# Attention, a feed-forward layer and capacity routing in one kernel: the float64 weights get a clock of their own

## The chip, the cores and the metric

One core of a Trainium2 chip runs the whole program. The metric is device time in microseconds for one execution, measured three times. TensorE multiplies matrices, VectorE, ScalarE and GpSimd do elementwise work, and SyncE issues most transfers; the profile calls them PE, DVE, ACT, POOL and SP, and the loading of TensorE's weights PEld.

## What is computed

```python
# attention: (4, 8, 1152, 64), query rows averaged in pairs -> 576 rows per head
q_pool = q.reshape(B, H, S // 2, 2, D).mean(axis=3)
scores = scale * np.matmul(q_pool, k.transpose(0, 1, 3, 2))
attn = softmax(scores);  x = np.matmul(attn, v)        # 32 heads -> x (2304, 512)
# feed-forward; moe_w_in and moe_w_out are float64
h = np.maximum(x @ w_in, 0.0);  x2 = h * h @ w_out     # 512 -> 2048 -> 512
# routing: 2304 tokens, 8 experts, capacity 288, largest logit first
logits = x2 @ w_gate
# then per expert: relu(x2[mask] @ w1[e]) @ w2[e]
```

## The kernel before

**Stages.** The 32 heads run one after the other (`Attention`, until about 758 us); the hidden layer of a batch of 8 heads runs between the steps of the next batch (`batch_h`), the last one alone (`last_h`, to 836 us). Then `Second` multiplies by w_out (72 groups of 12 products, `Second.product`), with the routing threaded between its products (`phase2`, to about 1085 us), and last come the eight experts (`MoE.run`). Products are made in two or three float32r parts of a high and a low half, which is why most tensors exist twice.

**A head** is 18 steps. Step g makes one score tile four steps ahead (`score`, L271: two products L278 and L279, then the exponential on ScalarE, L282). `events` (L355) hangs the preparation of later heads on steps by the table `AT` (L44): `q_sum` on GpSimd (L187), `q_high` on ScalarE (four copies a head, L195), `q_low` and `k_low` on GpSimd (L201, L178), transposes on TensorE (`k_turn`, `q_turn`) with casts by ScalarE or VectorE (L207, L225, L246), and 15 `peak` products (L263) with a maximum by VectorE each (L265). At a head's last step `av` (L294) emits 18 value products (L307, two records each) and the row sums, and behind them ScalarE copies the results out of two PSUM banks (L322, L324), the sums go to DRAM and back as a row (L327 to L340), and four to five steps later GpSimd normalises the head (`norm`, L485). Every engine takes its instructions strictly in the order of emission.

**Row sums.** For heads below `ADD_HEADS` = 11 TensorE sums the exponentials with 18 thin products (L319, 36 records); from head 11 on GpSimd adds the nine tiles up (`total`, L286, 16 additions L292 per head) and TensorE needs 2 (L313, 4 records).

**Float64 weights.** `F64.load` (L79) takes 64 parts of 128x256 values. Each is loaded (L87), then decoded by VectorE (L90, L96, L105) and ScalarE (L93, L99, L102), each piece hung on its own later step by `AT["f0"]` to `AT["f5"]`. A part of w_in is then split (ScalarE L433, GpSimd L437 twice); a part of w_out is turned on TensorE (L452), copied (L453), stored (L456), and every second one multiplied with the gate (L462). `between(g)` (L616) starts one part every `EVERY` = 4 steps from step `FROM` = -37, so that the last starts at step 215, in head 11. The work of the hidden layer starts `LAG` = 22 steps behind its batch (L620).

**PSUM.** The tiles named wx share three banks (`px`), scores another three, and h two. The value products, the row sums, transposes, peaks, the turned w_out and the gate all take wx.

**Routing.** The gate's logits of a half batch are summed in `ls` (`Half.logits`, L526) and stored to DRAM in four pieces (L540). `Routing.init` (L693) loads them back in three pieces (L699) and turns them with 18 products (L700, 36 records). `route` (L976) is a generator: each number that it yields is a count of w_out products to let pass, `START` = 36 before `init`, `FIRST` = 32 before the first digit of each of 5 iterations, and 16 or 8 elsewhere. A digit's counting products (L751) need VectorE's tile `G` (L740).

Of the kernel before, what the change touches and what calls it, by code (L numbers as in the profile page):

```python
# [10 lines left out]
F32 = mybir.dt.float32  # L11
# [3 lines left out]
AF = mybir.ActivationFunctionType  # L15
# [7 lines left out]
NQ = S // 2  # L23
# [10 lines left out]
EPS = 1e-9  # L34
LAG = 22
FROM = -37
EVERY = 4.0
ADD_HEADS = 11
LOGS = 3
# [5 lines left out]
AT = dict(lq=-55, qs=-43, lk=-50, qh0=-41, qh1=-41, ql=-38, kh0=-39, kh1=-37, kl=-36, kt0=-28, kt1=-28, kt2=-25,  # L45
          qt0=-25, t2=-22, pk=-23, lv=-12, qt1=-6, qt2=-6, total=5, recip=8, spread=9, norm=14,
          high=0, wlow=4, turn=3, keep=4, gate=5, f0=9, f1=9, f2=9, f3=11, f4=11, f5=14)
TL, TA = 1, 5
ITERS = 5
START, FIRST, FAST, SLOW, LAST = 36, 32, 8, 16, 14  # L50
ROUNDS = N // 48, 48, E
# [61 lines left out]
class Attention:  # L113
# [7 lines left out]
    def __init__(self, ctx, tc, cm, q, k, v, scratch, emit, px, ph, yp):  # L121
# [18 lines left out]
        self.st = {}  # L140
        self.now = 0
        self.later = []
        self.y, self.rb = {}, {}
# [45 lines left out]
    def q_high(self, n, i):  # L189
        d = self.st[n]  # L190
        qs = d["qs"]
        if i == 0:
            d["q1"] = self.q1[0]
        for p, c in self.PARTS:
            self.nc.scalar.activation(d["q1"][p, c, i * 64:(i + 1) * 64], qs[p, c], AF.Copy)  # L195

# [97 lines left out]
    def av(self, n):  # L294
# [26 lines left out]
        for hf in range(2):  # L321
            nc.scalar.activation(y[mine, hf * HQ:(hf + 1) * HQ], A[hf * 64:(hf + 1) * 64, :HQ], AF.Copy)  # L322
        row = self.w1.tile([128, HQ], F32, name="row")
        nc.scalar.activation(row, t[:, :HQ], AF.Copy, bias=EPS / parts)  # L324
        rc = self.w2.tile([96, 2, 6], F32, name="rc")
        for j in range(parts):
            nc.sync.dma_start(rc[:, j, :], row[j * 32:j * 32 + 65:64])  # L327
        for c in range(9):
            del d["P", c]

        def total():
            if parts == 2:
                nc.gpsimd.tensor_tensor(rc[:, 0], rc[:, 0], rc[:, 1], op=OP.add)

        def recip():
            nc.vector.reciprocal(rc[:, 0], rc[:, 0])

        def spread():
            nc.sync.dma_start(self.scratch[n:n + 1, :], rc[:, 0])
            nc.sync.dma_start(rb[mine, :], bass.AP(tensor=self.scratch.tensor,  # L340
                                                   offset=self.scratch.offset + n * NQ,
                                                   ap=[[0, 64], [1, NQ]]))

        self.at(AT["total"], total)
        self.at(AT["recip"], recip)
        self.at(AT["spread"], spread)
        if odd:
            for k, f in self.emit(pr, y, rb):
                self.at(k, f)
            del self.y[pr], self.rb[pr]  # L350

    def at(self, k, f):
        self.later.append((self.now + k, f))

    def events(self, n):  # L355
# [15 lines left out]

    def run(self, heads, between):
# [7 lines left out]
        while g < end or self.later:  # L380
            self.now = g
            if 0 <= g < end and g % L == L - 1:
                self.av(g // L)
            if g >= ORDER_FROM:
                between(g)
            if 0 <= g + self.AHEAD < end:
                self.score(*divmod(g + self.AHEAD, L))
            for t in [x for x in self.later if x[0] <= g]:
                self.later.remove(t)
                t[1]()  # L390
            for f, *a in todo.get(g, ()):
                f(*a)
            if g < ORDER_FROM:
                between(g)
            g += 1


@with_exitstack
def fused_kernel(ctx, tc, q, k, v, w_in, w_out, w_gate, w1, w2, out, dbg=None, upto=9):
# [98 lines left out]
    class Half:  # L498


        def __init__(self, b, hf, eng):
            self.tok = slice(b * NQ + hf * HQ, b * NQ + (hf + 1) * HQ)
            self.eng = eng
            self.X, self.group = [], []

        def product(self, p, f, parts):
# [19 lines left out]
        def logits(self, f0):  # L526

            lg = px.tile([128, 512], F32, name="wx")
            if f0 == 0:
                self.ls = hp.tile([128, HQ], F32, name="ls", bufs=1)  # L530
# [5 lines left out]
            else:  # L536
                nc.vector.tensor_tensor(ls, lg[:, :HQ], ls, op=OP.add)
            if f0 == NF - 4:
                for i in range(4):
                    nc.sync.dma_start(lgs[E * i:E * i + E, self.tok], ls[32 * i:32 * i + E])  # L540
# [27 lines left out]
    def last_h(b, es, beside, ahead):  # L568
# [15 lines left out]
        for hf in range(2):  # L584
            m = H[hf]
            for f in range(NF):
# [22 lines left out]
    with ExitStack() as ea:  # L609
        ea.enter_context(tc.manual_schedule())  # L610
        att = Attention(ea, tc, cm, q, k, v, rs_scr, emit_x, px, ph_, yp)
        raw = ea.enter_context(tc.tile_pool(name="raw", bufs=1))
        f64 = F64(tc, raw, att.at)
        parts, taken = setup(f64, raw), 0

        def between(g):  # L616
            nonlocal work, taken
            while taken * EVERY <= g - FROM and next(parts, 0) is None:
                taken += 1
            b, r = divmod(g - LAG, H * 18)  # L620
# [6 lines left out]

        att.run(NH, between)
        for _ in work:
# [16 lines left out]
class Routing:  # L646
    def __init__(self, ctx, tc, cm, lgs, psum):
# [44 lines left out]

    def init(self):  # L693
# [199 lines left out]
class Second:  # L893


    def __init__(self, ctx, tc, h2s, wos, x2s):
# [4 lines left out]
        self.hp = ctx.enter_context(tc.tile_pool(name="h2p", bufs=3, side="right"))  # L901
        self.px = ctx.enter_context(tc.tile_pool(name="x2_ps", bufs=2, space=PS, side="right"))
        self.woh = wp.tile([128, NF, DM], R, name="woh")
        self.wol = wp.tile([128, NF, DM], R, name="wol")
# [63 lines left out]
def phase2(ctx, tc, cm, sec, lgs, x2s, dbg, w1, w2, out, upto):  # L968
    nc = tc.nc
    mo = MoE(ctx, tc, cm, x2s, w1, w2, out)  # L970
    with ExitStack() as es:
# [4 lines left out]
        def route():  # L976
            yield START
            rt.init()
            for _ in range(ITERS):
# [216 lines left out]
```

## Time and profile before

| What | Value |
|---|---|
| median of 3 runs | 1330.46 us (1329.3 to 1331.21) |
| the profiled execution's own time | 1329.09 us |
| its span, first to last instruction | 1327.3 us |
| mean granted TensorE clock | 0.979 |
| busy PE / DVE / ACT / POOL | 1244.9 / 720.5 / 703.1 / 657.4 us |
| heads, end of the last one's sums | about 758 us |
| transfers | 155.57 MB, 117 GB/s in the mean |

A matmul's record holds its whole way through the array, and the next one overlaps it; so TensorE's busy share is high even where it is held up, and it is read together with the waits and with the spacing of the starts. Where a wait is shown, `<-` names the instruction that ended it. A timeline row is: start, length, engine, line, operation, tiles, count, and in brackets the idle time before it.

### The profile page before, as it was taken

The page shows a single profiled execution, that of the slowest core. Times are in us where ns is not written, and L with a number is a line of the kernel's source. Part 1 is how long each engine was busy: PE and PEld are TensorE (multiplying, and loading weights), DVE is VectorE, ACT ScalarE, POOL GpSimd, SP SyncE. Part 2 cuts the span into 40 slices and gives each one's busy share as a digit, 9 for nine tenths or more (in the row PEclk, how much of TensorE's full clock was granted, in tenths as well). Part 3 has the DMA queues.
Part 4 walks back from the last instruction along what each step waited for, and adds up shares of the span by engine and source line. Part 5 has one row for each costly group of instructions (what it writes and reads, how often), then busy time and mean ns, then how long its engine had stood idle before and what let it go on. Part 6 is the DMA issues. An engine that isn't in the chain of part 4 may idle for free. (4 is left out here: it accounts for less than half of the span.)

```text
span 1327.3 us, 25135 instructions
## 1 busy us (share of the span) xinstructions
PE 1244.9 (94%) x9033; PEld 1046.9 (79%) x9033; DVE 720.5 (54%) x1654; ACT 703.1 (53%) x1816; POOL 657.4 (50%) x930
## 2 busy tenths in 40 slices
PE   5898888989899999999999999999999979999997
PEld 4666665778688788887887889777777759999997
DVE  6867586666554445454544011178877714655552
ACT  5767675767566666566666556132322214454541
POOL 4332333356777878878877543366655301221211
PEclk9999999999999999999999999899999979999999
DMA  5444344443232323232322144444343314555531
GB/s 169 126 122 145 108 141 116 113 143 108 73 95 81 96 82 96 82 95 74 103 82 60 46 156 162 122 120 135 119 143 120 112 44 160 189 197 189 194 132 36
DMA packets 135096, 155.57 MB, mean 117 GB/s; under 512 B 17878, under 2 KB 95958, under 8 KB 134966
## 3 DMA queue, kind: packets, MB, share of 16 engines
q1 hardware_dynamic: 131750, 144.21, 35.7%
q0 software_dynamic: 3072, 9.44, 2.3%
q8 instruction: 73, 1.20, 0.4%
q14 instruction: 57, 0.47, 0.1%
q10 hardware_dynamic: 144, 0.26, 0.1%
HBM read 111.46 MB, written 32.87 MB: 109 GB/s over the span
## 5 line engine op out<-in xcount | busy, mean ns | idle before, releaser
L265 DVE TENSOR_REDUCE mx<-wx 128x1 f32<-128x384 f32 (+1 forms) x424 | 229.4, 551 | 244.9 <-PE wx L263 242.7
L282 ACT ACTIVATE P<-sc 128x288 f32<-128x288 f32 x576 | 225.1, 410 | 75.7 <-PE sc L279 68.6
L292 POOL TENSOR_TENSOR ss<-ss,P 128x288 f32<-128x288 f32 x294 | 229.3, 805 | 21.1 <-ACT P L282 20.6
L278 PE MATMUL sc<-M,T 128*128 128x288 f32 x576 | 178.3, 310 | 1.6 <-ACT P L282 1.4
L279 PE MATMUL sc<-M,t 128*128 128x288 f32 x576 | 171.6, 298 | 2.7 <-DVE M L246 2.6
L263 PE MATMUL wx<-T,M 128*128 128x384 f32 (+1 forms) x424 | 149.4, 352 | 7.6 <-ACT T L207 3.2
L935 POOL TENSOR_TENSOR hl<-h,hh 128x256 fp32r<-128x256 f32 x130 | 101.7, 804 | 109.6 <-ACT hh L933 106.0
L307 PE MATMUL wx<-P,vf 128*64 128x288 f32 x1152 | 147.7, 411 | 0.8 <-DVE mx L265 0.8
L512 PE MATMUL h<-xh,wih 128*128 128x288 f32 x448 | 140.1, 313 | 0.0
L512 PE MATMUL h<-xl,wih 128*128 128x288 f32 x448 | 134.2, 300 | 5.4 <-POOL xl L495 5.3
L512 PE MATMUL h<-xh,wil 128*128 128x288 f32 x448 | 132.9, 297 | 1.4 <-POOL wil L437 1.4
L307 PEld LDWEIGHTS wx<-P,vf 128*64 128x64 f32 x1152 | 80.3, 138 | 58.5 <-DVE mx L265 5.4
L278 PEld LDWEIGHTS sc<-M,T 128*128 128x128 f32 x576 | 109.5, 190 | 20.4 <-issue 7.4
L958 PE MATMUL x2p<-woh,hh 128*128 128x512 f32 x288 | 117.6, 408 | 0.0
L958 PE MATMUL x2p<-woh,hl 128*128 128x512 f32 x288 | 117.4, 408 | 0.0
L933 ACT ACTIVATE hh<-h 128x512 fp32r<-128x512 f32 x72 | 45.3, 630 | 135.7 <-PE x2p L958 130.6
L958 PE MATMUL x2p<-wol,hh 128*128 128x512 f32 x288 | 117.0, 406 | 0.0
L279 PEld LDWEIGHTS sc<-M,t 128*128 128x128 f32 x576 | 109.6, 190 | 4.9 <-DVE M L246 4.6
L512 PEld LDWEIGHTS h<-xh,wih 128*128 128x128 f32 x448 | 84.9, 190 | 10.2 <-issue 10.2
L178 POOL TENSOR_TENSOR ks<-raw,ks 128x192 fp32r<-128x192 f32 x93 | 55.5, 619 | 73.7 <-ACT ks L171 73.7
L512 PEld LDWEIGHTS h<-xl,wih 128*128 128x128 f32 x448 | 84.9, 189 | 8.8 <-POOL xl L495 8.7
L1070 POOL DMA_INDIRECT xg<-x_scr,ix x24 | 27.0, 1125 | 130.4 <-PE ept L1083 88.5
(199 smaller groups left out, 2937.8 us busy)
## 6 DMA issues: line engine op xcount, KB each, us to landing
eraw<-in_moe_w_dram SPq DMA_DIRECT2D x56, 512.0 KB
h_scr<-h2st SPq DMA_DIRECT2D x64, 288.0 KB
h<-h_scr SPq DMA_DIRECT2D x72, 256.0 KB
raw<-in_k_dram SPq DMA_DIRECT2D x32, 288.0 KB
t<-T SPq DMA_DIRECT2D x32, 288.0 KB
vf<-in_v_dram SPq DMA_DIRECT2D x32, 288.0 KB
raw<-in_q_dram SPq DMA_DIRECT2D x32, 256.0 KB
words<-in_moe_w_in_dram SPq DMA_DIRECT2D x32, 256.0 KB
```

The lines of the kernel that those rows point to most:

```text
L178: eng.tensor_tensor(ks[:, c, 0:64], d["kn"][:, c], ks[:, c, 64:128].bitcast(F32), op=OP.subtract)
L263: nc.tensor.matmul(t[:m, :384], d["M1"][:, c * 128:c * 128 + m], d["T1"][:, j * 384:(j + 1) * 384], start=True, stop=True)
L265: nc.vector.tensor_reduce(mx[:m, c, j:j + 1], t[:m, :384], axis=AX.X, op=OP.max)
L278: nc.tensor.matmul(t[:, :HQ], d["T1"][:, kk], d["M1"][:, qr], start=True, stop=False)
L279: nc.tensor.matmul(t[:, :HQ], d["T2"][:, kk], d["M2"][:, qr], start=False, stop=True)
L282: nc.scalar.activation(d["P", c][:, hf], t[:, :HQ], AF.Exp, scale=1.0 / (2.0 * math.sqrt(D)))
L292: self.nc.gpsimd.tensor_tensor(s, d["P", 0][:, hf] if c == 1 else s, d["P", c][:, hf], op=OP.add)
L307: nc.tensor.matmul(A[hf * 64:(hf + 1) * 64, :HQ], d["vf"][:, c], d["P", c][:, hf], start=(c == 0), stop=(c == 8))
L512: nc.tensor.matmul(p[:, :HQ], a[:, c, fs], x, start=(j == 0), stop=(j == 11))
L933: self.nc.scalar.activation(hh, t, AF.Copy)
L935: self.eng.tensor_tensor(hl[:, i:i + 2], t[:, i:i + 2], hh[:, i:i + 2].bitcast(F32), op=OP.subtract)
L958: nc.tensor.matmul(self.p, a[:, f, :], x[:, f0 + f, :], start=(f0 + f == 0 and i == 0), stop=(f0 + f == NF - 1 and i == 2))
```

## The change

Float64 work gets a clock of its own, `tick`: it counts every step and five more (`BURST`) for each head, which are taken between the emission of the value products and the copies behind them. A part starts every 4.5 ticks from tick -26. 23 ticks make a head. The rest: GpSimd makes `q_high` for heads 1 to 12; additions by GpSimd start at head 13 (`ADD_HEADS` 11 to 13; heads count from 0); `norm` moves from 14 to 18 steps behind and `LAG` from 22 to 24; the last half batch's logits stay in SBUF (`sec.ls`) together with the 96 columns before them, so that 15 of the 18 blocks come from DRAM, by one load that is issued when `Routing` is made; `START` is 14 and `FIRST` 38.

```diff
-LAG = 22
-FROM = -37
-EVERY = 4.0
-ADD_HEADS = 11
+LAG = 24
+FROM = -26
+EVERY = 4.5
+BURST = 5
+ADD_HEADS = 13
...
-          qt0=-25, t2=-22, pk=-23, lv=-12, qt1=-6, qt2=-6, total=5, recip=8, spread=9, norm=14,
-          high=0, wlow=4, turn=3, keep=4, gate=5, f0=9, f1=9, f2=9, f3=11, f4=11, f5=14)
+          qt0=-25, t2=-22, pk=-23, lv=-12, qt1=-6, qt2=-6, total=5, recip=8, spread=9, norm=18,
+          high=0, wlow=4, turn=3, keep=4, gate=5, f0=9, f1=9, f2=9, f3=11, f4=11, f5=13)
...
-START, FIRST, FAST, SLOW, LAST = 36, 32, 8, 16, 14
+START, FIRST, FAST, SLOW, LAST = 14, 38, 8, 16, 14
@@ q_high
-            self.nc.scalar.activation(d["q1"][p, c, i * 64:(i + 1) * 64], qs[p, c], AF.Copy)
+            o = d["q1"][p, c, i * 64:(i + 1) * 64]
+            if 0 < n < ADD_HEADS:
+                self.nc.gpsimd.tensor_copy(o, qs[p, c])
+            else:
+                self.nc.scalar.activation(o, qs[p, c], AF.Copy)
@@ av: what followed the products is now the function copies(), returned
+        return copies
@@ Attention
+    def beside(self, k, f):
+        self.side.append((self.tick + k, f))
+
+    def turn(self, supply):
+        self.tick += 1
+        supply(self.tick)
+        for t in [x for x in self.side if x[0] <= self.tick]:
+            self.side.remove(t)
+            t[1]()
@@ run
             if 0 <= g < end and g % L == L - 1:
-                self.av(g // L)
+                copies = self.av(g // L)
+                for _ in range(BURST):
+                    self.turn(supply)
+                copies()
...
             if g < ORDER_FROM:
                 between(g)
+            self.turn(supply)
             g += 1
@@ Half.logits
-            if f0 == 0:
+            if f0 == 0 and not self.last:
                 self.ls = hp.tile([128, HQ], F32, name="ls", bufs=1)
...
-            if f0 == NF - 4:
+            if f0 == NF - 4 and not self.last:
                 for i in range(4):
                     nc.sync.dma_start(lgs[E * i:E * i + E, self.tok], ls[32 * i:32 * i + E])
@@ last_h
+        H[1].last, H[1].ls = True, sec.ls[:, 3 * 128 - HQ:]
...
                     H[0].logits(NF - 4)
+                    nc.vector.tensor_copy(sec.ls[:, :3 * 128 - HQ], H[0].ls[:, 2 * HQ - 3 * 128:])
@@ fused_kernel
-        f64 = F64(tc, raw, att.at)
+        f64 = F64(tc, raw, att.beside)
...
+        def supply(tick):
+            nonlocal taken
+            while taken * EVERY <= tick - FROM and next(parts, 0) is None:
+                taken += 1
@@ Routing
+        self.quarters = cp.tile([128, E], F32, name="quarters")
+        nc.vector.tensor_reduce(self.quarters, cm.idf.rearrange("p (i x) -> p x i", x=32)[:, 0:E, :], axis=AX.X, op=OP.add)
+        self.lt = self.wk.tile([4 * E, (NC_T - 3) * 128], F32, name="lt")
+        nc.sync.dma_start(self.lt, lgs[:, :(NC_T - 3) * 128])
@@ Routing.init(ls)
-        for c in range(NC_T):
-            if c % 6 == 0:
-                lt = self.wk.tile([4 * E, 768], F32, name="lt", bufs=3)
-                nc.sync.dma_start(lt, self.lgs[:, c * 128:c * 128 + 768])
-            nc.tensor.matmul(p[:, c * E:(c + 1) * E], lt[:, c % 6 * 128:(c % 6 + 1) * 128], self.four,
+        for c in range(NC_T - 3):
+            nc.tensor.matmul(p[:, c * E:(c + 1) * E], self.lt[:, c * 128:(c + 1) * 128], self.four,
+                             start=True, stop=True)
+        for c in range(NC_T - 3, NC_T):
+            i = c - NC_T + 3
+            nc.tensor.matmul(p[:, c * E:(c + 1) * E], ls[:, i * 128:(i + 1) * 128], self.quarters,
                              start=True, stop=True)
```

## Rows read from the trace of the kernel before

**Rows 1.** The page: busy time of each engine, its share of the span, instructions.

```profile
PE 1244.9 (94%) x9033; PEld 1046.9 (79%) x9033; DVE 720.5 (54%) x1654; ACT 703.1 (53%) x1816; POOL 657.4 (50%) x930
```

**Rows 2.** Windows by stage: length, busy PE, PEld, DVE, ACT, POOL, granted clock, DMA, GB/s.

```profile
0.00:55.40 55.40, 36.91 (x227) 27.92 (x227) 39.76 (x95) 34.66 (x100) 22.61 (x43) 1.00 0.50 146
55.40:234.40 179.00, 159.81 (x1245) 116.45 (x1245) 125.26 (x309) 122.36 (x368) 57.83 (x112) 0.98 0.44 127
284.60:344.90 60.30, 52.03 (x373) 43.23 (x374) 40.85 (x68) 39.15 (x112) 38.22 (x58) 0.94 0.33 95
```

**Rows 3.** Windows: shorter stretches, columns as in rows 2.

```profile
14.20:26.50 12.30, 7.92 (x27) 4.86 (x25) 12.10 (x26) 7.61 (x22) 7.99 (x13) 1.00 0.66 198
141.60:157.30 15.70, 12.93 (x90) 11.27 (x90) 13.83 (x36) 13.66 (x43) 5.37 (x12) 1.00 0.61 175
157.30:164.40 7.10, 7.10 (x74) 3.70 (x73) 0.88 (x3) 1.90 (x6) 0.45 (x1) 1.00 0.03 9
258.70:284.60 25.90, 25.89 (x217) 21.45 (x218) 15.94 (x38) 19.01 (x57) 9.21 (x17) 1.00 0.48 148
366.40:388.70 22.30, 22.30 (x174) 19.20 (x173) 10.70 (x22) 13.96 (x40) 17.67 (x27) 1.00 0.32 88
846.00:856.50 10.50, 10.50 (x39) 9.27 (x39) 3.99 (x13) 0.43 (x1) 0.00 (x0) 0.51 0.13 37
```

**Rows 4.** Timeline of VectorE (DVE), heads 11 and 12: two long instructions.

```profile
291.79 4.61 DVE L90 TENSOR_SCALAR size<-words 128x256 int32<-128x256 int32 x1
...
331.99 6.02 DVE L105 TENSOR_TENSOR value<-sign,size 128x256 f32<-128x256 f32 x1
```

**Rows 5.** Timeline of GpSimd (POOL) in head 11: start, length, idle before.

```profile
302.54 0.79 POOL L292 TENSOR_TENSOR ss<-ss,P 128x288 f32<-128x288 f32 x1 [6.29 <-ACT P L282]
```

**Rows 6.** Waits between 836 and 1090 us: total, times, longest.

```profile
PE rps L751 <- DVE G L740: 4.1, 3, 2.1
```

**Rows 7.** Timeline of TensorE (PE) where routing begins.

```profile
840.62 0.39 PE L958 MATMUL x2p<-wol,hh 128*128 128x512 f32 x1
840.85 0.39 PE L958 MATMUL x2p<-woh,hl 128*128 128x512 f32 x1
...
844.53 6.37 PE L700 MATMUL rps<-four,lt 32*128 32x8 f32 x36 [3.30 <-DMA lt<-lg_scr]
```

**Rows 8.** Timeline of the first 30 us, all engines.

```profile
7.54 0.33 PE L223 MATMUL wx<-idr,q 128*128 128x128 f32 x1
...
10.60 0.44 ACT L93 ACTIVATE sign<-words 128x256 f32<-128x256 f32 x1 [4.38 <-DMA words<-in_moe_w_in_dram]
...
10.94 1.08 ACT L207 ACTIVATE T<-wx 128x512 fp32r<-128x512 f32 x2
```

**Rows 9.** Groups by line: count, busy us, mean ns, idle before and releasers.

```profile
L96 DVE SCALAR_TENSOR_TENSOR size<-words,size 128x256 int32<-128x256 int32 x64 | 38.5, 602 | 2.2
...
L105 DVE TENSOR_TENSOR value<-sign,size 128x256 f32<-128x256 f32 x64 | 36.0, 562 | 3.7 <-DMA wo_scr<-value 1.4 <-ACT sign L99 1.3 <-ACT size L102 0.7
...
L187 POOL TENSOR_TENSOR qs<-raw 128x256 f32<-128x256 f32 x64 | 33.7, 545 | 4.0 <-DMA raw<-in_q_dram 3.9
...
L195 ACT ACTIVATE q<-qs 128x256 fp32r<-128x256 f32 (+1 forms) x128 | 32.3, 326 | 8.9 <-POOL qs L187 8.9
...
L90 DVE TENSOR_SCALAR size<-words 128x256 int32<-128x256 int32 x64 | 29.3, 457 | 3.7 <-DMA words<-in_moe_w_in_dram 3.7
...
L319 PE MATMUL wx<-P,ones 128*32 128x288 f32 x396 | 28.8, 409 | 0.0
...
L313 PE MATMUL wx<-ss,ones 128*64 128x288 f32 x84 | 13.8, 406 | 0.0
```

**Rows 10.** Timeline near 31 us: GpSimd and VectorE side by side.

```profile
31.07 1.29 POOL L201 TENSOR_TENSOR q<-qs,q 128x256 fp32r<-128x256 f32 x2 [1.46 <-ACT q L195]
...
31.34 0.84 DVE L96 SCALAR_TENSOR_TENSOR size<-words,size 128x256 int32<-128x256 int32 x1
```

**Rows 11.** Timeline where the heads end: first product of the last batch.

```profile
776.65 0.40 PE L512 MATMUL wx<-xh,wih 128*128 128x288 f32 x1 [2.90 <-ACT xh L494]
```

More of the change, by code (lines that the diff above doesn't have):

```diff
@@ L140, in __init__ @@
         self.st = {}
-        self.now = 0
-        self.later = []
+        self.now = self.tick = 0
+        self.later, self.side = [], []
         self.y, self.rb = {}, {}
@@ L320, in av @@
                                      start=(c < 2), stop=(c > 6))
[L321 to L327, printed above, removed]
         for c in range(9):
@@ L329, in av @@
             del d["P", c]
[L331 to L350, printed above, removed]
+        def copies():
+            for hf in range(2):
+                nc.scalar.activation(y[mine, hf * HQ:(hf + 1) * HQ], A[hf * 64:(hf + 1) * 64, :HQ], AF.Copy)
+            row = self.w1.tile([128, HQ], F32, name="row")
+            nc.scalar.activation(row, t[:, :HQ], AF.Copy, bias=EPS / parts)
+            rc = self.w2.tile([96, 2, 6], F32, name="rc")
+            for j in range(parts):
+                nc.sync.dma_start(rc[:, j, :], row[j * 32:j * 32 + 65:64])
+            def total():
+                if parts == 2:
+                    nc.gpsimd.tensor_tensor(rc[:, 0], rc[:, 0], rc[:, 1], op=OP.add)
+            def recip():
+                nc.vector.reciprocal(rc[:, 0], rc[:, 0])
+            def spread():
+                nc.sync.dma_start(self.scratch[n:n + 1, :], rc[:, 0])
+                nc.sync.dma_start(rb[mine, :], bass.AP(tensor=self.scratch.tensor,
+                                                       offset=self.scratch.offset + n * NQ,
+                                                       ap=[[0, 64], [1, NQ]]))
+            self.at(AT["total"], total)
+            self.at(AT["recip"], recip)
+            self.at(AT["spread"], spread)
+            if odd:
+                for k, f in self.emit(pr, y, rb):
+                    self.at(k, f)
+                del self.y[pr], self.rb[pr]
@@ L370, in events, with run @@
         return ev
-    def run(self, heads, between):
+    def run(self, heads, between, supply):
         L = self.STEPS
@@ L379, in run @@
         g, end = min(todo), heads * L
-        while g < end or self.later:
+        self.tick = g
+        while g < end or self.later or self.side:
             self.now = g
             if 0 <= g < end and g % L == L - 1:
-                self.av(g // L)
+                copies = self.av(g // L)
+                for _ in range(BURST):
+                    self.turn(supply)
+                copies()
             if g >= ORDER_FROM:
@@ L504, in __init__ @@
             self.X, self.group = [], []
+            self.last = False
         def product(self, p, f, parts):
@@ L612, in fused_kernel @@
         raw = ea.enter_context(tc.tile_pool(name="raw", bufs=1))
-        f64 = F64(tc, raw, att.at)
+        f64 = F64(tc, raw, att.beside)
         parts, taken = setup(f64, raw), 0
         def between(g):
-            nonlocal work, taken
-            while taken * EVERY <= g - FROM and next(parts, 0) is None:
-                taken += 1
+            nonlocal work
             b, r = divmod(g - LAG, H * 18)
@@ L626, in between @@
                 next(work, None)
-        att.run(NH, between)
+        def supply(tick):
+            nonlocal taken
+            while taken * EVERY <= tick - FROM and next(parts, 0) is None:
+                taken += 1
+        att.run(NH, between, supply)
         for _ in work:
@@ L691, in bc_c, with init @@
         return a[:, None, :].to_broadcast([128, NC_T, E])
-    def init(self):
+    def init(self, ls):
         nc = self.nc
         p = self.psum.tile([128, 512], F32, name="rps")
-        for c in range(NC_T):
-            if c % 6 == 0:
-                lt = self.wk.tile([4 * E, 768], F32, name="lt", bufs=3)
-                nc.sync.dma_start(lt, self.lgs[:, c * 128:c * 128 + 768])
-            nc.tensor.matmul(p[:, c * E:(c + 1) * E], lt[:, c % 6 * 128:(c % 6 + 1) * 128], self.four,
+        for c in range(NC_T - 3):
[4 more added lines that the diff above has]
+            nc.tensor.matmul(p[:, c * E:(c + 1) * E], ls[:, i * 128:(i + 1) * 128], self.quarters,
                              start=True, stop=True)
@@ L902, in __init__ @@
         self.px = ctx.enter_context(tc.tile_pool(name="x2_ps", bufs=2, space=PS, side="right"))
+        self.ls = wp.tile([128, 3 * 128], F32, name="lslast")
         self.woh = wp.tile([128, NF, DM], R, name="woh")
@@ L977, in route @@
             yield START
-            rt.init()
+            rt.init(sec.ls)
             for _ in range(ITERS):
```

## The prediction

> **What bounds the kernel now.** First the page: TensorE is busy for 94% of the span and no other engine for more than 54% [rows 1]. A record of TensorE runs on while the engine waits, so this says only that TensorE should set the pace wherever nothing holds it; where it is held must be read by stage. The windows give the stages [rows 2]: the first 55.4 us, with TensorE busy for 36.9; heads 1 to 8, 179 us or 22.4 each, though they carry no hidden-layer products yet; heads 11 and 12, 60.3 us. Shorter windows say what holds them [rows 3]. Head 14, with hidden-layer products and without float64 work, takes 22.3 us, all of them TensorE's: the floor of a full head. In head 5, without those products, the steps ahead of the value products take 15.7 us, with VectorE busy for 13.83, ScalarE for 13.66 and TensorE for 12.93: two engines that work in order are nearly full, and the float64 decoding is part of both. Then come 7.1 us of value products and sums, in which VectorE works 0.88 us and ScalarE 1.90. That is the hole that the burst is to fill.
>
> Heads 11 and 12 are something else. There one VectorE instruction takes 4.61 us and another 6.02 [rows 4], where such work otherwise takes about half a microsecond. The first ends at 296.40; GpSimd's own row after it starts at 302.54 behind 6.29 us of idle time [rows 5], so GpSimd had stopped at 296.25, after additions and float64 pieces without a break. Two things overlap in these heads alone: GpSimd's additions and float64 work.
>
> In the routing stage TensorE waits for VectorE's G three times, 4.1 us together, the longest 2.1 [rows 6], and 3.30 us for the logits' load [rows 7].
>
> **The change, part by part.**
>
> *Start.* The transposes of head 0 end at 7.87 us, yet the cast behind them starts at 10.94, since ScalarE stands before it with the first float64 piece, whose load lands at 10.60 [rows 8]. With FROM -26 that piece comes eleven steps later, behind the cast: about 3.0 us. From 14.2 to 26.5 VectorE is busy for 12.10 of 12.30 us [rows 3], so float64 pieces cost there what they last. A part costs VectorE 0.457 + 0.602 + 0.562 = 1.62 us [rows 9]. Before, eleven parts are decoded by step 12 (from step -28, one every 4); after, seven by tick 13 (from -17, one every 4.5). Four parts fewer are 6.5 us of VectorE; I take 4, as TensorE and ScalarE also carry something once scores run. Start: -7 us, between -3 (the load alone) and -9.5.
>
> *Heads 1 to 8.* In 18 steps there were 4.5 parts; now there are 18/4.5 = 4.0, and 5/4.5 = 1.1 go beside the value products. VectorE loses 0.5 x 1.62 = 0.8 us a head there. ScalarE loses half a part too, and the four q_high copies, 32.3/32 = 1.0 us [rows 9]. Those go to GpSimd. No row shows a GpSimd copy: below stands ScalarE's 1.0 us for the four, above four additions of the same shapes by GpSimd, 4 x 0.545 = 2.2 us [rows 9]. I take 1.5, between the two, since the copy has one input and the addition two. What it costs is not GpSimd's time, which is free here (57.8 of 179 us [rows 2]), but VectorE's: beside GpSimd's 1.29 us an instruction of L96 takes 0.84 us [rows 10], against 0.602 in the mean [rows 9]. Float64 work fills 4 x 1.62 of 15.7 us, or 41%, so 1.5 us of copies meet 0.6 us of it and cost about 0.3. TensorE gets 0.6 part more a head, some 0.1 to 0.2 us. Net -0.4 us a head, -3 in all. The bounds: if the three engines are all freed, heads fall to TensorE's 12.93 + 7.1 = 20.0 us, -19; if the copies each hold VectorE for their whole length, +0.7 a head, +6.
> The Trainium skill (GPSIMD Engine Reference, section 8, Key points) speaks against this part: GpSimd shares its SBUF interfaces with VectorE, and instructions with two SBUF inputs or in a two-port mode contend. Rows 10 agree in kind: the instruction beside GpSimd was slowed and not stopped; rows 4 show that it can be stopped. By the rule at its strictest this part's term would be +6, by the slowed row it is -3.
>
> *The burst's own cost.* The copies behind the value products now stand on ScalarE behind up to five ticks of pieces. These run while TensorE still multiplies, except the copy of a turned w_out part, which waits for TensorE; with it two of the three wx banks stay taken about a microsecond longer. Costed at nothing: the next scores have banks of their own. Without that cover it is 1 us in each head whose burst holds a turn, seven of twelve: the +6 to +7 is within the bound above.
>
> *Heads 9 to 12.* Float64 work now ends near the end of head 11, and additions begin at head 13, so they no longer meet. Head 10 shows what a head costs with hidden-layer products, float64 work and TensorE's sums: 25.9 us [rows 3]. Head 12 without float64 work is head 14 plus the sums on TensorE, 28.8/11 - 13.8/21 = 2.0 us [rows 9]: 24.3. Together 50.2 in place of 60.3 [rows 2], -10; a little more float64 work in heads 9 and 10 gives 1 back: -9. Bounds: the two long instructions alone, 10.6 us less their ordinary length, -9.6, and everything but half of that, -4; with heads 9 and 10 drawn in, -12.
>
> *Norm and LAG.* Norm is moved past steps whose GpSimd work doesn't wait for it, at no cost: the last head of a batch is normalised by step 19 of the next, and the batch starts at step 24. LAG leaves two more units of three products for the gap after the last head, where TensorE waits 2.90 us for the last normalised head [rows 11]; it shortens the full heads by as much. 6 x 0.13 us: -0.8, between 0 and -2.9.
>
> *Routing.* The 3.30 us wait goes: the logits that it waited for never leave SBUF, and one load of old rows is issued ahead of the expert weights and four stores. The 36 records of the turn stay. They last 6.37 us [rows 7], and from 846 to 856.5 the granted clock is 0.51 [rows 3], the lower of the two levels (1.2 of 2.4 GHz), right behind the wait and among these thin products: 10.5 x 0.49 = 5.1 us lost. I take half of it as saved, 2.6: the wait is gone, the thin products aren't. FIRST gives G six more products of 0.23 us [rows 7], 1.4 us: of 4.1 us of waits 0.7 stay, from the longest, -3.4; and some 0.7 for clock lost after that one. START less 22 and FIRST more by 30 are 8 products more in all, 746 in place of 738: the routing ends in the 63rd group of twelve, not the 62nd, and the dispatch still fits ahead of the 72nd. Sum -10, between -5 (the load's wait only partly gone, the clock as now) and -13.5.
>
> *Sum.* -7 - 3 - 9 - 0.8 - 10 = -29.8 on the profiled execution's 1329.1 us gives 1299.3; the median of the runs is 1.4 above that execution, so 1300.7, say **1301 us**.
>
> **Rivals.**
> *The burst frees the in-order engines fully.* Heads 1 to 8 fall to TensorE's 20.0 us: -19 in place of -3, **1285 us**. For it: both engines are idle for most of 7.1 us. Against: four parts in 4.5 stay in the steps, and VectorE stays at some 13 of 15 us. Chance 0.16.
> *The routing keeps its holes.* The load still comes late for the earlier START, and the clock drops as now among thin products: half of -10 is lost, **1306 us**. For it: START leaves only 14 x 0.23 = 3.2 us. Chance 0.20.
> *Heads 11 and 12 stay long.* Something other than additions made VectorE stand still, for GpSimd also split weights and normalised there: -9 is lost, **1310 us**. Here the change would not do what it says. Against: GpSimd was idle for 6.29 us from the moment on that the long instruction ended [rows 5]. Chance 0.10.
> *Slower: GpSimd's trains move into heads 1 to 12.* q_sum, four copies and q_low now stand on GpSimd without ScalarE's answer between them: 1.1 + 1.5 + 1.1 us. If a VectorE float64 instruction is held for the whole train, as in rows 4, each of 12 heads loses 3.2 us, +38 against -29.8: **1339 us**. It decides from 2.5 us a head on. For it: rows 4; against: rows 10, where a train of 1.29 us cost 0.4. Chance 0.06.
>
> **How the numbers follow.** My forecast has 0.48. The range 1283 to 1316 takes in the three faster rivals and the bounds of the terms, and leaves out the slower one and the extremes of several terms at once. About 0.2%, 2.7 us, is what a measurement of this kernel can tell from no change. Faster by more: 0.91; within it, where the trains eat the gain: 0.03; slower: 0.06.
>
> **What would show it.** Head 0's sums end near 48 us, not 55; heads 1 to 8 take about 22 us each; no VectorE float64 instruction lasts over 2 us, and heads 11 and 12 take about 26 and 24; TensorE has no wait for the logits' load, at most one for G, and a shorter stretch at the lower clock near 840 to 855. Wrong would be: trains on GpSimd with VectorE instructions of 3 us beside them, TensorE waiting for ScalarE's copies of the value products, or a wait for the load within routing.

## The result and the profile after

The changed kernel takes **1311.8 us** in the median of four runs (1309.6 to 1314.0), beside 1329.9 for the kernel before: a ratio of 0.9855 [0.9819, 0.989], 18 us less. The sign and the range were right; the time is 11 us above the forecast of 1301. The profiled execution took 1313.98 us, with a span of 1312.2.

The page of the changed kernel, busy time of each engine, as in [rows 1]:

```profile
PE 1247.6 (95%) x9097; PEld 1047.8 (80%) x9097; DVE 705.9 (54%) x1654; ACT 695.7 (53%) x1768; POOL 644.2 (49%) x950
```

Nothing there tells the story; the stages do. Windows of the changed kernel (columns as in [rows 2]): head 0, heads 1 to 8, 9 and 10, 11 and 12, 13 to 31, from there to the first w_out product, w_out with the routing, experts:

```profile
0.00:52.90 52.90, 38.95 (x222) 29.93 (x222) 35.95 (x86) 29.45 (x79) 24.91 (x53) 0.94 0.50 136
52.90:239.80 186.90, 167.30 (x1265) 122.57 (x1263) 130.91 (x327) 124.47 (x357) 69.41 (x148) 0.95 0.45 131
239.80:291.50 51.70, 46.96 (x387) 37.67 (x386) 32.19 (x75) 38.57 (x115) 20.12 (x39) 1.00 0.43 128
291.50:343.60 52.10, 51.88 (x431) 42.67 (x432) 26.24 (x59) 33.81 (x98) 12.22 (x23) 1.00 0.33 98
343.60:755.90 412.30, 408.44 (x3097) 343.12 (x3097) 188.56 (x394) 261.69 (x733) 323.64 (x467) 1.00 0.29 84
755.90:828.00 72.10, 69.16 (x517) 62.45 (x517) 9.96 (x23) 42.92 (x100) 26.03 (x29) 0.98 0.46 151
828.00:1067.40 239.40, 238.12 (x1459) 184.25 (x1457) 160.17 (x516) 61.60 (x105) 118.64 (x144) 0.99 0.41 123
1067.40:1312.20 244.80, 226.80 (x1730) 225.09 (x1728) 121.88 (x176) 103.21 (x185) 49.22 (x48) 0.97 0.48 152
```

The same stages of the kernel before and of two kernels of the experiments below, in us. A head is cut where ScalarE begins to copy its row sums out of PSUM (L324 before, L333 after):

| Stage | before | after | copies on ScalarE | and early reciprocal | forecast change |
|---|---|---|---|---|---|
| head 0 | 55.4 | 52.9 | 48.9 | 48.7 | -7 |
| heads 1 to 8 | 179.0 | 186.9 | 180.4 | 180.1 | -3 |
| heads 9 to 12 | 110.5 | 103.8 | 103.1 | 103.7 | -9 |
| heads 13 to 31 | 413.0 | 412.3 | 412.3 | 412.3 | 0 |
| to the first w_out product | 71.3 | 72.2 | 72.5 | 68.7 | -0.8 |
| w_out with routing | 252.8 | 239.3 | 239.6 | 239.6 | -10 |
| experts | 245.1 | 244.8 | 244.7 | 245.1 | 0 |

With the burst this copy comes late, 1.5 to 2.9 us behind the last product of the sums in seven of heads 0 to 12; in the kernel before it comes at most 0.4 us behind. So part of a difference between before and after is the place of the cut. Cut at the end of the sums' last product instead:

| Stage | before | after | copies on ScalarE |
|---|---|---|---|
| head 0 | 55.4 | 51.4 | 47.3 |
| heads 1 to 8 | 179.0 | 185.6 | 179.1 |
| heads 9 to 12 | 110.1 | 106.6 | 105.9 |

Head 0, heads 9 to 12 and the routing gained, the routing more than forecast, head 0 a third of it (4.0 of 7 by the sums' ends); heads 1 to 8 **lost** 7.9 us (6.6 by the sums' ends) where 3 were to be gained.

Each stage is read from one profiled execution. How far it repeats is shown by kernels whose code is the same there: heads 1 to 8 take 186.9, 186.3 and 186.2 us with the burst and GpSimd's copies (after, experiments 4 and 7), 180.4, 180.1 and 178.8 with the burst and ScalarE's (1, 8 and 9), 179.0 and 181.4 without either (before, 3).

**Heads 1 to 8.** The granted clock of this stage fell from 0.98 [rows 2] to 0.95. Timeline of the changed kernel, 175.6 to 179.8 us, GpSimd, VectorE and TensorE:

```profile
175.67 1.21 POOL L198 CAST q<-qs 128x256 fp32r<-128x256 f32 x4 [3.51 <-PE wx L250]
...
176.17 0.68 DVE L251 CAST M<-wx 128x512 fp32r<-128x512 f32 x1
...
176.77 1.78 DVE L91 TENSOR_SCALAR size<-words 128x256 int32<-128x256 int32 x1
176.84 0.86 POOL L462 TENSOR_TENSOR wil<-value,wih 128x128 fp32r<-128x128 f32 x2
...
177.67 1.04 POOL L206 TENSOR_TENSOR q<-qs,q 128x256 fp32r<-128x256 f32 x2
...
178.93 0.68 DVE L251 CAST M<-wx 128x512 fp32r<-128x512 f32 x1
...
179.66 0.69 PE L268 MATMUL wx<-T,M 128*128 128x384 f32 x1 [2.07 <-DVE M L251]
```

From 175.67 to 178.71 GpSimd works without a gap: four copies, two splits, two more subtractions. The VectorE piece L91, 0.286 us in its median here, lasts 1.78 and ends at 178.55, as GpSimd is about to. Behind it stands the cast that TensorE needs: TensorE waits 2.07 us. Within that wait the clock falls to its lower level (1.2 of 2.4 GHz); the window of the stretch at that level:

```profile
178.50:185.30 6.80, 5.64 (x22) 4.07 (x24) 5.62 (x15) 3.03 (x8) 2.17 (x4) 0.50 0.57 165
```

The copies start where they do because they wait for the transposes of the head before. GpSimd's groups by line in heads 1 to 8 (count, busy us, mean ns, idle before and its releaser):

```profile
L198 POOL CAST q<-qs 128x256 fp32r<-128x256 f32 (+1 forms) x32 | 9.8, 345 | 19.8 <-PE wx L250 19.8
```

The copies themselves are cheaper than estimated, 4 x 0.345 = 1.4 us a head for 1.5; but the transposes that release them also release VectorE's casts, so the two engines begin together each time.

**Start.** The cast behind head 0's transposes moved up as told: in the kernel before it starts at 10.94 [rows 8]. Timeline of the changed kernel, first 10 us:

```profile
6.93 1.27 ACT L212 ACTIVATE T<-wx 128x512 fp32r<-128x512 f32 x3 [0.93 <-PE wx L226]
...
7.33 0.33 PE L228 MATMUL wx<-idr,q 128*128 128x128 f32 x1
```

The gain is spent later in head 0, timeline of the same kernel at 36 to 39 us:

```profile
36.21 1.27 POOL L198 CAST q<-qs 128x256 fp32r<-128x256 f32 x4 [1.73 <-PE wx L250]
...
36.91 1.54 DVE L97 SCALAR_TENSOR_TENSOR size<-words,size 128x256 int32<-128x256 int32 x1
...
38.93 0.34 PE L253 MATMUL wx<-idr,q 128*128 128x128 f32 x1 [2.22 <-DVE M L232]
```

Again copies (those of head 3 by now), a held VectorE piece and a TensorE wait; from 38.5 to 45.3 us the granted clock is 0.50.

**Routing.** Timeline of TensorE where the logits are turned, and the wait for G, in the changed kernel, for [rows 6, 7]:

```profile
834.93 4.48 PE L733 MATMUL rps<-four,lt 32*128 32x8 f32 x30
839.34 1.45 PE L737 MATMUL rps<-quarters,lslast 128*128 128x8 f32 x6
```

```profile
PE rps L788 <- DVE G L777: 1.2, 1, 1.2
```

The 3.30 us wait [rows 7] is gone and one of three G waits is left, 1.2 us for 4.1 [rows 6].

**The gap after the last head** stayed: 2.94 us for 2.90 [rows 11]. Timeline of the changed kernel there:

```profile
766.79 0.46 DVE L563 TENSOR_TENSOR ls<-wx,ls 128x288 f32<-128x288 f32 x1 [1.44 <-PE wx L559]
...
767.16 0.18 DVE L343 RECIPROCAL rc<-rc 96x6 f32<-96x6 f32 x1
...
775.49 0.40 PE L538 MATMUL wx<-xh,wih 128*128 128x288 f32 x1 [2.94 <-ACT xh L519]
```

The last head's reciprocal (L343) stands on VectorE behind the sum of logits (L563), which waits 1.44 us for a product of the very hidden-layer units that LAG moved.

### The profile page after: what moved, and what is told of

Read it like the earlier page. It is cut to its first block, busy times and chain, and to the rows that moved or that the text cites. A ratio compares the mean times of both kernels' runs of the same rounds, so it can differ in the third digit from the quotient of the medians.

```text
span 1312.2 us, 25163 instructions
## 1 busy us (share of the span) xinstructions
PE 1247.6 (95%) x9097; PEld 1047.8 (80%) x9097; DVE 705.9 (54%) x1654; ACT 695.7 (53%) x1768; POOL 644.2 (49%) x950
## 5 line engine op out<-in xcount | busy, mean ns | idle before, releaser
L297 POOL TENSOR_TENSOR ss<-ss,P 128x288 f32<-128x288 f32 x266 | 206.1, 806 | 4.1 <-ACT P L287 3.0
L283 PE MATMUL sc<-M,T 128*128 128x288 f32 x576 | 183.0, 318 | 2.6 <-ACT P L287 2.1
L312 PE MATMUL wx<-P,vf 128*64 128x288 f32 x1152 | 151.1, 418 | 0.0
L971 ACT ACTIVATE hh<-h 128x512 fp32r<-128x512 f32 x72 | 45.3, 630 | 126.4 <-PE x2p L996 114.1
L179 POOL TENSOR_TENSOR ks<-raw,ks 128x192 fp32r<-128x192 f32 x93 | 55.4, 618 | 88.8 <-ACT ks L172 88.8
L538 PEld LDWEIGHTS h<-xh,wih 128*128 128x128 f32 x444 | 83.6, 188 | 10.2 <-issue 10.2
```

Source lines behind the costliest of these rows:

```text
L283: nc.tensor.matmul(t[:, :HQ], d["T1"][:, kk], d["M1"][:, qr], start=True, stop=False)
L297: self.nc.gpsimd.tensor_tensor(s, d["P", 0][:, hf] if c == 1 else s, d["P", c][:, hf], op=OP.add)
L312: nc.tensor.matmul(A[hf * 64:(hf + 1) * 64, :HQ], d["vf"][:, c], d["P", c][:, hf], start=(c == 0), stop=(c == 8))
L538: nc.tensor.matmul(p[:, :HQ], a[:, c, fs], x, start=(j == 0), stop=(j == 11))
```

## The experiments

The theory was that GpSimd's copies cost the missing time, by holding VectorE pieces that stand ahead of casts TensorE waits for; the rivals, that the burst or the denser pieces cost it.

**1. The copies back on ScalarE**, all else as changed.

```diff
-            if 0 < n < ADD_HEADS:
+            if False:
```

> Theory: q_high on GpSimd costs heads 1 to 8 more than the burst gives, because its four copies, the split pieces and q_low now follow one another without a break and hold VectorE's float64 pieces, which stand ahead of the casts that TensorE waits for. With the copies back on ScalarE, and all else of the change kept, heads 1 to 8 fall from 186.9 us to about 176, no VectorE float64 instruction lasts over 1.2 us, and the time is about 1302 us. Rival: the pieces are simply denser (5.1 parts a head for 4.5), and the copies do not matter: heads 1 to 8 stay within 183 to 190 us and the time within 3 us of the changed kernel's 1311.8.

Measured: 1302.5 us (1301.0 to 1306.9), ratio to the kernel before 0.9791 [0.9732, 0.985], 9.3 us under the changed kernel. Head 0 takes 48.9 us, heads 1 to 8 180.4. Windows of this kernel, those two stages:

```profile
0.00:48.90 48.90, 36.19 (x222) 27.80 (x223) 34.57 (x86) 31.50 (x92) 21.44 (x41) 1.00 0.54 147
48.90:229.30 180.40, 163.53 (x1264) 119.92 (x1263) 129.73 (x327) 129.92 (x389) 59.27 (x116) 0.97 0.47 135
```

And sizes of the VectorE piece (min, median, max in ns), this kernel:

```profile
L91 DVE TENSOR_SCALAR size<-words x64: 273/285/902, 13.1 to 296.8; 128x256 int32<-128x256 int32 x64
```

The longest of these is 0.90 us, and no VectorE piece of float64 work is over 0.98. The time came out as the theory said; the stage, 180.4, fell short of its 176. Group by line, heads 1 to 8, first of the changed kernel, then of this one:

```profile
L91 DVE TENSOR_SCALAR size<-words 128x256 int32<-128x256 int32 x41 | 17.0, 415 | 0.0
```

```profile
L91 DVE TENSOR_SCALAR size<-words 128x256 int32<-128x256 int32 x41 | 14.7, 359 | 2.0 <-DMA words<-in_moe_w_out_dram 2.0
```

The copies cost that group 2.3 us over eight heads, 0.3 a head; over all VectorE work of the stage 130.91 - 129.73 = 1.2 us. The stage loses 6.5. The rest is where the delay falls: TensorE's waits for L251 sum to 4.9 us in the changed kernel's stage and 2.5 here, the longer of them, first of the changed kernel, then of this one:

```profile
PE sc L284 <- DVE M L251: 2.4, 2, 1.8
...
PE wx L268 <- DVE M L251: 2.1, 1, 2.1
```

```profile
PE sc L284 <- DVE M L251: 1.4, 2, 1.0
...
PE wx L268 <- DVE M L251: 0.7, 1, 0.7
```

And the stage holds 20.5 us at the lower clock for 10.2 here, at half speed at most 5.1 us more. The two together, 2.4 + 5.1 = 7.5, are enough for it, and the clock is the larger part. The kernel before has 6.8 us at the lower clock in this stage, so against it too the clock is at most 6.8 of the 7.9.

**2. The copies alone in the kernel before**, the same edit the other way.

```diff
+            o = d["q1"][p, c, i * 64:(i + 1) * 64]
+            if 0 < n < 13:
+                self.nc.gpsimd.tensor_copy(o, qs[p, c])
```

> The kernel before with one edit: q_high on GpSimd for heads 1 to 12. Theory (the copies on GpSimd hold VectorE's float64 pieces with or without the burst): heads 1 to 8 rise from 179.0 us to 184 to 190, VectorE float64 instructions of over 1.2 us appear in them, the time is 4 to 12 us longer than before. Rival (the copies hurt only together with the burst, which brings pieces to where the copies stand): heads 1 to 8 stay at 177 to 181 us and the time within 2 us of before, or under it as ScalarE is freed of 1.0 us a head.

Measured: 1340.1 us, 1.0067 [1.0041, 1.0092], and 184.8 us for heads 1 to 8 in place of 179.0. Timeline of this kernel:

```profile
93.94 1.16 POOL L197 CAST q<-qs 128x256 fp32r<-128x256 f32 x4
...
94.52 3.77 DVE L96 SCALAR_TENSOR_TENSOR size<-words,size 128x256 int32<-128x256 int32 x1
...
95.07 1.14 POOL L489 TENSOR_TENSOR y<-y,rb 128x192 f32<-128x192 f32 x2
96.18 1.00 POOL L205 TENSOR_TENSOR q<-qs,q 128x256 fp32r<-128x256 f32 x2
97.14 0.86 POOL L441 TENSOR_TENSOR wil<-value,wih 128x128 fp32r<-128x128 f32 x2
97.97 0.77 POOL L178 TENSOR_TENSOR ks<-raw,ks 128x192 fp32r<-128x192 f32 x1
```

Eleven GpSimd instructions without a gap from 93.94 on, and one VectorE instruction of 0.43 us held from 94.52 to 98.29. This part of the change alone makes the kernel slower.

**3. Additions from head 13 alone, in the kernel before.**

```diff
-ADD_HEADS = 11
+ADD_HEADS = 13
```

> The kernel before with one edit: additions by GpSimd from head 13. Theory (the two long VectorE instructions come from additions that meet float64 work): heads 11 and 12 fall from 60.4 us to 51 to 53, no VectorE float64 instruction lasts over 2 us, the time is 7 to 10 us shorter than before. Rival (they come from GpSimd's other work there, as in the run with additions from head 11, which cost no time): heads 11 and 12 stay at 57 us or more, or the 4 us that TensorE pays for two more heads of sums eat the gain; the time is within 3 us of before.

Measured: 1324.4 us, 0.9939 [0.9917, 0.9961]. Window of heads 11 and 12 of this kernel, 60.3 before:

```profile
288.40:341.30 52.90, 52.02 (x435) 43.08 (x435) 29.15 (x68) 38.65 (x112) 14.34 (x27) 1.00 0.37 109
```

The heads gave what was forecast, 7.4 us, the time only 5.1 for the 7 to 10: in its profile heads 1 to 10, which this edit does not touch, are longer by 4.9. Window of these heads in this kernel:

```profile
54.40:288.40 234.00, 214.84 (x1639) 161.77 (x1640) 156.69 (x381) 160.68 (x483) 76.66 (x145) 0.95 0.43 125
```

The granted clock is 0.95 there, 0.99 in the kernel before: 23.9 us at the lower level for 6.8, at most 8.5 us, which is enough for the 4.9. Why the clock fell more often is open.

**4. Additions from head 11 in the changed kernel**, copies as changed.

```diff
-ADD_HEADS = 13
+ADD_HEADS = 11
...
-            if 0 < n < ADD_HEADS:
+            if 0 < n < 13:
```

> Additions by GpSimd from head 11 again, q_high on GpSimd for heads 1 to 12 kept. Theory (additions that meet float64 work hold VectorE): float64 work runs to the end of head 11, so head 11 gets a VectorE float64 instruction of 3 us or more, heads 11 and 12 take 55 to 58 us for 52.1, and the time is 3 to 6 us longer. Rival (additions were not the cause): heads 11 and 12 take 48 to 50 us, as TensorE saves 2.0 us in each, and the time is 2 to 4 us shorter.

Measured: 1312.5 us (0.9858 [0.9802, 0.9914]), the time of the changed kernel; heads 11 and 12 take 52.8 us for 52.1. Timeline of head 11 in this kernel:

```profile
297.94 3.07 POOL L297 TENSOR_TENSOR ss<-ss,P 128x288 f32<-128x288 f32 x4
...
297.96 3.75 DVE L97 SCALAR_TENSOR_TENSOR size<-words,size 128x256 int32<-128x256 int32 x1
```

A long instruction is back, once. It costs about what 2 us less of sums on TensorE in each of the two heads give. So neither theory holds whole: once float64 work ends in head 11, the later start of the additions is worth nothing that shows.

**5. The changed kernel without the burst**, a part every 3.5 steps so that float64 work ends at about the same step.

```diff
-EVERY = 4.5
-BURST = 5
+EVERY = 3.5
+BURST = 0
```

> No burst, and a part every 3.5 steps in place of 4.5 ticks, so that float64 work ends at about the same step (212 for 216). Theory (the burst gives what was forecast for it): 5.1 parts a head now all stand in the steps, 1.1 more than with the burst, 1.8 us of VectorE a head: heads 1 to 8 take 195 to 202 us for 186.9, the time is 1318 to 1326 us. Rival (the burst itself costs, by late copies behind the value products or by bunched pieces): heads 1 to 8 take 175 to 183 us, the time is 1300 to 1307.

Measured: 1318.8 us, 0.992 [0.989, 0.9949], within the theory's range; heads 1 to 8 take 190.6 us, under its 195 to 202.

**6. The same with the copies on ScalarE** (the edit of 1 added):

> The changed kernel with q_high on ScalarE and without the burst, a part every 3.5 steps: the burst alone, free of GpSimd's copies, against the run with q_high on ScalarE (1302.5 us; head 0 48.9, heads 1 to 8 180.4, heads 9 to 12 103.1 us). Theory (the burst takes 1.1 parts a head out of the steps, 1.6 us of VectorE each, about half of it on the path): heads 1 to 8 take 185 to 193 us, the time is 1307 to 1315 us. Rival (what the burst hides it loses by the late copies): heads 1 to 8 within 3 us of 180.4, the time within 4 us of 1302.5.

Measured: 1308.3 us, 0.9826 [0.978, 0.9873]. Window of heads 1 to 8 of this kernel, 180.4 with the burst:

```profile
50.80:236.80 186.00, 166.35 (x1257) 121.63 (x1257) 129.73 (x326) 128.97 (x387) 59.68 (x117) 0.95 0.45 131
```

The burst is worth 5.6 us in heads 1 to 8 and 5.8 in the time, 3.7 and 6.9 with the copies on GpSimd (6.9 and 5.0 in the stage by the sums' ends). The size is rough: single runs of 1 and of 6 overlap (1301.0 to 1306.9 and 1304.9 to 1310.8). It pays for 18/3.5 = 5.1 parts a head in place of 4.5 (18/4.0), and for no more that shows: with copies on ScalarE heads 1 to 8 take 180.4 us for the 179.0 of the kernel before, 179.1 for 179.0 by the sums' ends.

**7. START and FIRST as before.**

```diff
-START, FIRST, FAST, SLOW, LAST = 14, 38, 8, 16, 14
+START, FIRST, FAST, SLOW, LAST = 36, 32, 8, 16, 14
```

> START 36 and FIRST 32 again, the last logits still kept in SBUF. Theory (the six more products cover G): TensorE's waits for G return to about 4 us from 1.2, the w_out stage (first to last product) takes about 243 us for 239.3, with the clock lower once more in it; the time is 3 to 5 us longer. Rival (the missing load alone made the gain): the stage stays within 1 us of 239.3 and the time too.

Measured: 1315.8 us (1313.4 to 1320.9), 0.988 [0.9823, 0.9936]. Waits of this kernel in the stage:

```profile
PE rps L788 <- DVE G L777: 4.2, 4, 1.4
```

The waits for G are back, 4.2 us for 1.2, and the median is 4.0 higher. The stage takes 246.4 us for 239.4, with a second stretch at the lower clock, 6.8 us from 1056.4 on; but the profiled execution, 1320.9 us, is the longest of the four.

**8. The last head's reciprocal early**, on top of 1.

```diff
-            self.at(AT["recip"], recip)
-            self.at(AT["spread"], spread)
+            last = n == B * H - 1
+            self.at(1 if last else AT["recip"], recip)
+            self.at(2 if last else AT["spread"], spread)
```

> The changed kernel with q_high on ScalarE, and for the last head the reciprocal and the spread of the sums emitted 1 and 2 steps behind its value products in place of 8 and 9. Theory (two more units in the gap gave nothing because the reciprocal stands on VectorE behind the logits of those same units): TensorE's wait of 2.9 us for the last normalised head goes, with the stretch of lower clock behind it; from the last head's sums to the first w_out product 67.5 to 69.5 us for 72.5, the time 1297 to 1299 us for the 1302.5 of the run with q_high on ScalarE. Rival (the way of the sums through DRAM is as long as the cover): the wait stays over 1.5 us and the time within 1.5 us of 1302.5.

Measured: 1300.2 us, 0.9778 [0.9739, 0.9818]. Timeline of this kernel:

```profile
747.06 0.19 DVE L343 RECIPROCAL rc<-rc 96x6 f32<-96x6 f32 x1 [11.50 <-DMA rc<-row]
```

The reciprocal now waits for its row alone; the gap is gone and the stretch to the first w_out product falls from 72.5 to 68.7 us, as the theory said. The median fell by 2.3, less than the 3.5 to 5.5 of the theory, and less than the runs of 1 scatter.

**9. Additions from head 12**, on top of 8, to balance TensorE and GpSimd.

```diff
-ADD_HEADS = 13
+ADD_HEADS = 12
```

> As the run with the early reciprocal, with additions from head 12 in place of 13. Theory (only float64 work that meets additions costs; it ends in head 11): head 12 falls from 24.5 us to about 22.5, head 11 stays at 27.6, the time is 1 to 3 us shorter than that run's. Rival (the last pieces still meet the first additions, which start four steps ahead): a VectorE instruction of over 2 us at the end of head 11 and the time no shorter.

Measured: 1303.5 us (1298.5 to 1306.6), 0.9777 [0.9745, 0.9809]; heads 11 and 12 take 50.4 us for 52.1. But head 29 takes 28.6 us for 21.6. Timeline of head 29 in this kernel:

```profile
692.48 8.95 DVE L521 TENSOR_TENSOR xl<-y,xh 128x288 fp32r<-128x288 f32 x1 [0.84 <-ACT xh L520]
...
696.56 4.55 POOL L297 TENSOR_TENSOR ss<-ss,P 128x288 f32<-128x288 f32 x6
...
701.94 0.75 PE L250 MATMUL wx<-idr,q 128*128 128x128 f32 x4 [6.12 <-DVE mx L270]
```

VectorE's subtraction L521, 0.544 us in its median here, lasts 8.95, beside subtractions and additions of GpSimd that follow one another without a gap until 701.11. Behind it stands the maximum that TensorE waits 6.12 us for. In experiment 8, with the same code there, no L521 of VectorE is over 0.87 us. So this is the hold of experiments 2 and 4 once more, without any float64 work. The heads in question gained 1.7 us, as told, and the hold took more than that back; whether the shorter of the six runs are without it is not shown, so what the edit is worth stays open.

**10. A burst of eight ticks with parts every 5**, on top of 8.

```diff
-EVERY = 4.5
-BURST = 5
+EVERY = 5.0
+BURST = 8
```

> The run with the early reciprocal (1300.2 us, heads 1 to 8 180.1 us) with BURST 8 and EVERY 5.0: 26 ticks a head, 1.6 parts beside the value products for 1.1, 3.6 in the steps for 4.0, float64 work over at about the same head. Theory (the hole of 7 us is not yet full): heads 1 to 8 take 174 to 178 us, the time is 1294 to 1298 us. Rival (the hole is full: ScalarE's copies behind the value products come later instead): heads 1 to 8 take 180 us or more, the time is no shorter than 1299 us.

Measured: **1298.4 us** (1297.1 to 1301.9), 0.9768 [0.9721, 0.9816], the shortest median of all. Window of heads 1 to 8 of this kernel:

```profile
47.40:227.10 179.70, 161.96 (x1253) 116.42 (x1252) 128.41 (x325) 130.00 (x389) 60.21 (x117) 0.99 0.47 136
```

179.7 us for 180.1: the stage did not shorten, and 1.8 us in the median lies within the scatter of both. Inconclusive as to the burst's length; as a version it beats the changed kernel by 13 us and the one before by 30.

## Why the prediction was right and where it failed

**Heads 1 to 8: the step that failed**, +7.9 where -3 stood (+6.6 by the sums' ends). One half of it is the price of GpSimd's copies, "cost about 0.3" a head. Counted as VectorE time that price was about right in this kernel (0.3 a head on L91, 0.15 on all of VectorE, experiment 1), in part by luck: the 0.602 us that it took for the ordinary length of L96 is a mean that holds slowed ones. Sizes of L96 in the kernel before (min, median, max in ns):

```profile
L96 DVE SCALAR_TENSOR_TENSOR size<-words,size x64: 424/428/1799, 10.9 to 326.6; 128x256 int32<-128x256 int32 x64
```

By the median the 0.84 of [rows 10] is twice the ordinary length, and the same working gives 0.6 a head. What the price left out is the path: a held float64 piece stands on VectorE ahead of the casts of the transposes, TensorE waits for these, and its clock falls in or behind the wait. So 1.2 us of VectorE time became 6.5 us of the stage, at most 5.1 of it by the clock, and in all the copies cost 9.3 us of the median. The upper bound, "+6", was a bound on VectorE's time too, and so fell short of the term that came out. The Trainium skill (GPSIMD Engine Reference, section 8, Key points) names VectorE instructions with two SBUF inputs or in a two-port mode as those that contend with GpSimd; the trace agrees for L97, which has two inputs and was held to 1.54 us, and for the cast L251 out of PSUM, which took 0.68 us beside the copies at 176.17 and 0.68 without them at 178.93. L91, with one input, was held to 1.78 us; in which mode it ran no run here shows. That section of the Trainium skill gives no length for the contention; [rows 4] and experiment 2 show most of a train, 3.77 to 6.02 us.

**The other half of that term** was -0.8 a head for VectorE's pieces taken out of the steps, less 0.1 to 0.2 for TensorE: some -5 in eight heads. Without the copies the stage is 1.4 us above the kernel before (0.1 by the sums' ends), so this half missed by 5 us or more, the copies' half by 4.1 (6.5 for 8 x 0.3 = 2.4). The burst does fill the hole (5.6 us), but the denser pieces that it was paired with take as much: the 0.8 us a head of VectorE that was counted as freed does not show in the length of the stage. ScalarE may have a part in it, since in experiment 1 it keeps the 1.0 us of copies a head that the forecast had taken off it; no run separates that. VectorE's busy time there rose, 129.73 us for 125.26 [rows 2], since 41 parts are begun in it for 36.

**The burst's own cost** was put at nothing. The copies behind the value products come 1.5 to 2.9 us late in seven heads, where about one microsecond in seven of twelve was told, but no wait of TensorE for them is over 0.24 us in the changed kernel. What else they cost is not separated from the burst's gain.

**Start**, -2.5 for -7 (-4.0 by the sums' ends, at 51.4 for the 48 told). The step holds: with the copies off GpSimd it is 55.4 - 48.9 = -6.5 (-8.0). What was not counted is that the copies of heads 1 to 3 run in the stage of head 0; they took 4.0 back.

**Heads 9 to 12**, -6.7 for -9 (-3.5 by the sums' ends, since head 8's late copy then counts to these heads): heads 11 and 12 take 27.6 and 24.5 us, 26.0 and 26.1 by the sums' ends, 52.1 together for the 50.2 worked out. Both long instructions are gone. But experiment 4 narrows the reason. In the kernel before, the later start of the additions gave 7.4 us of these heads by itself (experiment 3); in the changed kernel, where float64 work ends in head 11, it gives nothing that shows. That the earlier end of the float64 work did most of it there is argued from this; no run tried it alone.

**Norm and LAG**, nothing for -0.8. The term took the normalised head as fixed in time and the products as cover. In fact the normalisation hangs on a reciprocal that stands on VectorE behind logits of the same products; experiment 8 moves it and gets 3.8 us, more than the whole gap.

**Routing**, -13.5 for -10: the mechanism was right and the term too small, at the bound named for it. START and FIRST give about 4 of it (experiment 7; -3.4 and -0.7 were counted). The stretch at the lower clock is 6.8 us long at 837 where it was 10.2 at 846, 1.7 us at half speed where 2.6 stood. What is left of the excess the clock can account for. Windows of the kernel before, the stage and two more stretches in it:

```profile
829.30:1082.10 252.80, 245.11 (x1458) 189.27 (x1457) 165.16 (x518) 61.57 (x105) 120.92 (x142) 0.96 0.39 117
975.80:979.20 3.40, 3.40 (x10) 2.24 (x9) 2.81 (x7) 1.15 (x2) 2.03 (x3) 0.50 0.27 79
1064.60:1071.40 6.80, 6.80 (x37) 5.60 (x36) 0.39 (x2) 0.67 (x2) 0.00 (x0) 0.50 0.00 0
```

Neither stretch is left in the changed kernel, whose clock is 0.99 in the stage: at most 5.1 us, where 0.7 was counted. With 3.3 for the load's wait, 2.9 for G and the 1.7 this makes 13.0. The first stretch stands behind the longest wait for G. The second falls among the thin products of the dispatch (L884), behind no wait; the like of it is in three of the four kernels with START 36 and in none of the eight with START 14. Why it comes there is open.

**The rivals.** The slower one named the mechanism that cost 9.3 of the 11 us between forecast and time. It was to decide from 2.5 us a head on; the copies cost heads 1 to 8 0.8 a head, so it bent the time and did not turn it. "The burst frees fully" falls with experiments 6 and 10. The sign set to show trains, VectorE instructions of 3 us, was too coarse: the longest float64 piece was 1.78 and the loss was there. The total of experiment 1, 1302.5, is close to the forecast, partly by chance, since routing gave 3 more and heads 1 to 12 gave 6 less than their terms.

## What to carry to other kernels

The clock is part of a wait's price: a short wait can cost more by the lower clock around it than by its own length. An idle engine is no free place for work: price a moved instruction by what the neighbour that it slows has queued behind it, and by whether TensorE waits for that, not by the neighbour's busy time. A chain of small GpSimd instructions is safer with another engine's step between its links, even one that is not needed there, than unbroken; that is argued from the holds, no run tests the break by itself. Test the parts of a change apart: here one part of six gave back a third of what the others gained.

## What the runs showed of the hardware

A VectorE instruction of 0.3 to 0.6 us that reads SBUF can last to near the end of GpSimd's unbroken run of instructions, within half a microsecond: 1.78 and 3.77 us beside trains of copies and subtractions, 3.75 beside four additions and a subtraction, 8.95 beside additions and subtractions in experiment 9, 4.61 and 6.02 in the kernel before [rows 4]. The 0.84 us of [rows 10], which the prediction calls slowed, need not be another kind: of GpSimd's two subtractions the first ends at 31.90 and the VectorE instruction at 32.19, so it may have been held for the first alone. Why a hold ends behind one instruction or lasts for many these runs do not settle.

TensorE's waits of 2.22 and 2.07 us in the changed kernel each had the clock at its lower level for 6.8 us, from within the wait on (38.5 and 178.5 us): up to 3.4 us of work lost, more than the wait. Two waits of 2.24 and 2.32 us in experiment 2 had it there for 3.4 us each (from 69.2 and 157.9 us).
